# Turning attention probabilities on VectorE and by transfer instead of on TensorE, in a block-sparse attention with a channel-mix layer

## The chip, the core and the metric

One core of one Trainium2 chip runs the whole program. The metric is the device time of one execution in microseconds; lower is better. The median of three runs of the kernel before is 576.97 us (575.19 to 577.18).

## What is computed

Batch 4, 8 heads, 768 positions, head size 64, in float32. Attention is block-sparse with blocks of 32 positions (24 blocks): a query block sees the first and the last block, itself and its two neighbours, and three sampled blocks; the first and last query blocks see everything. What follows is a channel-mix layer over 512 channels with 1024 hidden units.

```python
mask = np.abs(blk_i - blk_j) <= 1
mask = mask | (blk_i == 0) | (blk_j == 0) | (blk_i == 23) | (blk_j == 23)
for qb in range(24):
    for kb in sampled_blocks[qb]:
        mask[qb*32:(qb+1)*32, kb*32:(kb+1)*32] = True
scores = np.where(mask, 0.125 * (q @ k.T), -1e9)
attn = np.exp(scores - scores.max(-1)); attn = attn / attn.sum(-1)
x = (attn @ v).transpose(0, 2, 1, 3).reshape(4, 768, 512)
xk = mu_k * x + (1 - mu_k) * x_prev      # x_prev: x one position earlier
xr = mu_r * x + (1 - mu_r) * x_prev
k = np.maximum(xk @ w_k, 0)
out = sigmoid(xr @ w_r) * (k * k @ w_v)
```

## The kernel before

**Units and tiles.** Attention runs as 24 units, counted from 0: two wide ones (the first and last query blocks of a pair of batches, `load_wide`, `wide_pair`) and 22 gathered ones (`load_near`, `near_unit`), each for two query blocks of two batches, so that 128 partitions are 4 x 32 queries. In names, `s_8_1` is the scores of gathered unit 8 of its batch pair, head group 1. The channel mix runs over 12 tiles of 128 positions (two batches each): `gate` (matmuls `r`), `hidden` or `hidden_of_two` (`h`) and `values` (`v`), each product as three float32r terms.

**A gathered unit.** For each of two groups of four heads: 32 small matmuls write scores `s` to PSUM (L609); four VectorE instructions (`soft`, L558) add the mask, take the minimum of the negated scores and write to `p` in SBUF; four ScalarE instructions (`exp`, L567) put exponentials in place. `p` has queries on its partitions, and the product with V needs keys there, so `turn` transposes it: TensorE transposes four 128x128 blocks into a PSUM tile `t` (L578), VectorE copies that tile to `pt` (L584), twice per group. Then 64 small matmuls (L640) multiply by V. From unit 8 on (`MERGE`) both groups' scores are one planned step, and so are both products. `finish` (L692) divides by the sums and transposes the result into the channel mix's input.

The softmax writes `p` through two views, and that order decides which partition a probability has after the transposition:

```python
dealt = lambda x: x.rearrange("p (g x a) -> p x a g", g=2, a=QB)
```

**Buffers.** One key buffer (`KR_BUFS` 1), six value buffers (two pairs in use per unit), four `p` buffers (`P_BUFS`), four `pt`, two PSUM tiles `t`, one PSUM bank `m` for the channel mix's results (`BANKS`; the last five tiles take more).

**The order.** Each step goes to `plan.add(engine, ns, rank, fn, reads, writes, ...)`. `Plan.order` places steps by a model of engines, buffers and transfers, and among those that can start takes the lowest rank; each engine then runs its steps strictly in the order that comes out. Ranks come from tables (`UNIT_AT`, `TILE_AT`) and offsets (`O_TR`, `LEAD_K`, ...). All loads and stores of the steady part are issued by SyncE (SP), in the planned order too; a transfer that has to wait holds up those behind it.

Of the kernel before, what the change touches and what calls it, by code (L numbers as in the profile page):

```python
# [19 lines left out]
P = 128  # L20
# [6 lines left out]
TT = 128  # L27
# [244 lines left out]
def block_sparse_attention_channel_mix(  # L272
# [31 lines left out]
    near_mask = fixed([P, NM, SLOTS], F32, "near_mask")  # L304
# [9 lines left out]
    def mask_setup():  # L314
# [21 lines left out]
        def twice():  # L336
            v = nc.vector
            c = con.ap[:, near:].bitcast(F32)
            v.tensor_copy(out=near_mask.ap, in_=c[:, NM * SEEN :].rearrange("p (a b) -> p a b", b=SLOTS))
# [13 lines left out]
            m = near_mask.ap[:, :, 0 : 2 * NRAND - 1 : 2]  # L353
            v.scalar_tensor_tensor(out=m, in0=s_, scalar=-FAR, in1=m, op0=ALU.mult, op1=ALU.add)

        plan.add(DVE, 2900, TWICE, twice, reads=[(con,)], writes=[(f,), (same,), (near_mask,)])
# [20 lines left out]
    def weight(i, owner, key, dst, src, rank):  # L377
        f = buf([P, 512], F32, "zr", Z_BUFS, f"wf{i}")
        if wide:
            raw = Part(early, EARLY_W, lambda x, i: x[:, 1024 * i : 1024 * (i + 1)].bitcast(I32).rearrange("p (a b) -> p a b", b=2)) if i < 3 * CC else buf([P, 512, 2], I32, "p", P_BUFS, f"raw{i}")  # L380
            mag = buf([P, 512], F32, "kk", 2, f"wmag{i}")
            at = RAW_AT + RAW_GAP * i if i < 3 * CC else rank
# [45 lines left out]
    def weights():  # L428
# [9 lines left out]
        for i, job in enumerate(jobs):  # L438
            late = i - 3 * CC
            weight(i, *job, rank=W0 + W1 * i + (V0 + V1 * late if late >= 0 else 0.0))  # L440
# [22 lines left out]
    def load_wide(pr, at, step):  # L463

        q = buf([P, HP, P], F32, "q", 2, f"qw{pr}")
        lead = (pr, ALL) == UNITS[0]
        for lo, hi in ((0, 1), (1, HP)) if lead else ((0, HP),):
            plan.add(SP, ISSUE, -60 + 1.5 * lo if lead else at - LEAD_Q, lambda lo=lo, hi=hi: nc.sync.dma_start(q.ap[:, lo:hi], qw[pr, :, lo:hi]),
                     writes=[(q, *range(lo, hi))], release=at - LEAD_Q, size=wire(65536 * (hi - lo), 512 * (hi - lo)))
        keys, values = [], []  # L470
        for hp in range(HP):
            keys.append([])
            values.append([])
            for i in range(PAIR):
                r = Part(k_ring, K_RING, lambda x, i: x[:, i])
                keys[-1].append(r)
                due = -59 + hp + 0.1 * i if lead else at + step * hp - LEAD_W
                if lead and not hp:
                    half = S // 2
                    for h in range(2):  # L480
# [6 lines left out]
                         writes=[(r, 0), (r, 1)], release=due, size=wire(393216, 3072))  # L487
            for i in range(PAIR):
                r = Part(v_ring, V_RING, lambda x, i: x[:, i])
                values[-1].append(r)  # L490
                due = -58.5 + hp + 0.1 * i if lead else at + step * hp - LEAD_X
                plan.add(SP, ISSUE, due, lambda r=r, hp=hp, i=i: nc.sync.dma_start(r.ap, vw[pr, hp, :, i]),
                         writes=[(r,)], release=due, size=wire(393216, 3072))
        return q, keys, values

    def load_near(pr, m, at):
# [5 lines left out]
        ahead = FIRST_K if (pr, m) == (0, 0) else LEAD_K  # L502
# [507 lines left out]

T_ACT = ((0, 1, 2), (2,))

BANKS = [("m", M_BUFS)]
LAST, XT_BUFS = 5, 6
WARM = 10
MERGE = 8
# [92 lines left out]
```

## Time and profile before

| | |
|---|---|
| median of 3 runs | 576.97 us |
| the profiled execution | 577.41 us, of which its span (first to last instruction) 575.5 us |
| TensorE busy | 541.6 us, 94% |
| VectorE, ScalarE, GpSimd busy | 302.0, 283.9, 301.8 us (49 to 52%) |
| transfers | 108.50 MB; the main queue 56.1% of 16 engines' span |

A busy share says how long an engine had work in it. Whether more could go through it is read from what it did between. A group of matmuls in the timeline starts while the one before it drains, so its cost is the distance from its start to the next start, not its own duration.

### The profile page before, as it was taken

How to read it: one execution, taken by the hardware profiler on the slowest of the kernel's cores; microseconds unless marked ns; L12 is line 12 of the kernel's file. 1: busy time of each engine (PE TensorE's matmuls, PEld its weight loads, DVE VectorE, ACT ScalarE, POOL GpSimd, SP SyncE). 2: the span in 40 equal slices, each digit the busy share in tenths (PEclk: the TensorE clock that was granted, in tenths of full speed). 3: DMA queues.
4: the chain of work that ended last, by engine and by line, in shares of the span. 5: the costliest groups of instructions: out<-in, count | busy, mean ns of one | idle time of the engine just before them, and what ended most of it. 6: DMA issues, size and time to landing. Idle time of an engine off the chain costs nothing.

```text
span 575.5 us, 18197 instructions
## 1 busy us (share of the span) xinstructions
PE 541.6 (94%) x7139; PEld 441.1 (77%) x7139; DVE 302.0 (52%) x818; ACT 283.9 (49%) x703; POOL 301.8 (52%) x368
## 2 busy tenths in 40 slices
PE   7978657898999999999999999999999999999997
PEld 3555434787789779888878888878989888888886
DVE  1887787877777673755467455556222313232001
ACT  3576664468366752744646455565324243422520
POOL 0067544868547345444406644415717879767820
PEclk8999787998999999999999999999999999999999
DMA  8999989998877887875785655484320000000001
GB/s 329 338 363 351 331 305 298 303 308 253 298 231 235 258 268 226 248 229 190 222 273 159 200 185 187 159 272 115 119 83 21 19 20 0 19 36 19 0 19 55
DMA packets 53942, 108.50 MB, mean 189 GB/s; under 512 B 9505, under 2 KB 28578, under 8 KB 53858
## 3 DMA queue, kind: packets, MB, share of 16 engines
q1 hardware_dynamic: 53570, 106.96, 56.1%
q8 instruction: 56, 0.92, 0.6%
q10 hardware_dynamic: 288, 0.39, 0.2%
q14 instruction: 28, 0.23, 0.1%
HBM read 100.77 MB, written 6.55 MB: 187 GB/s over the span
## 4 chain that ended last, share of the span: by engine, by line
PE 75%; DMA 6%; DVE 3%; SPq 2%; issue 1%; POOL 1%
PE v L898 23%; PE o L640 7%; PE s L609 5%; PE t L578 5%; PE r_1p L838 5%; PE h_3p L864 4%; PE r_0p L838 4%; PE h_0p L864 4%; PE h_1p L864 4%; PE h_2p L864 4%; DMA VR<-vt 2%; DMA KR<-kt 2%; DMA VR<-vn 1%; PE tx L703 1%; DVE p L558 1%; PE h_2p L880 1%
## 5 line engine op out<-in xcount | busy, mean ns | idle before, releaser
L898 PE MATMUL v<-wv,k 128*128 128x512 f32 (+1 forms) x600 | 140.9, 389 | 0.0
L898 PEld LDWEIGHTS v<-wv,k 128*128 128x128 f32 x600 | 108.2, 188 | 26.8 <-issue 1.2
L567 ACT ACTIVATE p<-p,nm 128x256 f32<-128x256 f32 x176 | 87.3, 498 | 31.4 <-DVE nm L558 31.2
L558 DVE CUSTOM_DVE_ANT_1 p<-s,near_mask 128x256 f32<-128x256 f32 x176 | 89.7, 632 | 19.2 <-PE s L609 19.0
L584 DVE COPY pt<-t 128x512 f32<-128x512 f32 x88 | 59.1, 686 | 67.2 <-PE t L578 54.1
L578 PE MATMUL t<-ident,p 128*128 128x128 f32 x352 | 52.0, 279 | 7.1 <-DVE pt L584 3.7
L640 PE MATMUL o<-VR,pt 128*32 128x64 f32 x2816 | 48.6, 228 | 5.9 <-DMA VR<-vt 5.1
L640 PEld LDWEIGHTS o<-VR,pt 128*32 128x32 f32 x2816 | 44.2, 115 | 11.5 <-issue 6.2
L578 PEld LDWEIGHTS t<-ident,p 128*128 128x128 f32 x352 | 41.5, 143 | 14.8 <-ACT ptw L582 3.9
L609 PE MATMUL s<-KR,q 64*32 64x256 f32 x1408 | 48.8, 402 | 4.3 <-DMA KR<-kt 4.3
L814 POOL TENSOR_TENSOR xr<-xr_1f,xr 128x256 fp32r<-128x256 f32 x24 | 17.9, 745 | 58.6 <-ACT xr L812 58.1
L805 DVE SCALAR_TENSOR_TENSOR xr_1f<-xr_1d,mk,xt 128x128 f32<-128x128 f32 x48 | 18.3, 423 | 50.3 <-POOL xr L814 42.8
L906 DVE SCALAR_TENSOR_TENSOR z<-v,z 128x512 f32<-128x512 f32 (+1 forms) x25 | 16.8, 671 | 52.8 <-PE v L898 36.8
L609 PEld LDWEIGHTS s<-KR,q 64*32 64x32 f32 x1408 | 27.5, 111 | 18.1 <-issue 5.8
L805 DVE SCALAR_TENSOR_TENSOR xr_0f<-xr_0d,mk,xt 128x128 f32<-128x128 f32 x48 | 20.0, 457 | 26.2 <-POOL xr L814 15.9
L567 ACT ACTIVATION_READ_ACCUMULATOR p<-p,nm 128x1 f32 x176 | 32.9, 187 | 0.0
L838 PE MATMUL r_0p<-wr,xr 128*128 128x512 f32 x120 | 31.2, 404 | 0.0
L838 PE MATMUL r_1p<-wr,xr 128*128 128x512 f32 x120 | 30.5, 401 | 0.0
L801 POOL TENSOR_TENSOR xr_0d<-xt 128x128 f32<-128x128 f32 x48 | 20.3, 442 | 18.0 <-DVE xr_0f L805 5.2
L814 POOL TENSOR_TENSOR xr<-xr_0f,xr 128x256 fp32r<-128x256 f32 x24 | 17.7, 738 | 21.1 <-ACT xr L812 21.1
L558 DVE DVE_READ_ACCUMULATOR2_ANT nm<- 128x1 f32 x176 | 28.3, 161 | 0.0
L812 ACT CAST xr<-xr_1f 128x256 fp32r<-128x256 f32 x24 | 9.7, 405 | 35.4 <-PE r_0p L838 16.9
(168 smaller groups left out, 1005.3 us busy)
## 6 DMA issues: line engine op xcount, KB each, us to landing
VR<-vn SPq DMA_DIRECT2D x44, 512.0 KB, 4.8
VR<-vt SPq DMA_DIRECT2D x138, 128.0 KB, 3.8
KR<-kt SPq DMA_DIRECT2D x132, 128.0 KB, 3.5
KR<-kd SPq DMA_DIRECT2D x22, 512.0 KB, 5.1
v_ring<-vw SPq DMA_DIRECT2D x16, 384.0 KB, 5.8
out<-z SPq DMA_DIRECT2D x23, 256.0 KB, 2.2
q<-qn SPq DMA_DIRECT2D x22, 256.0 KB, 3.8
k_ring<-kw SPq DMA_DIRECT2D x14, 384.0 KB, 6.4
```

The source lines that it names most:

```text
L558: nc.vector.tensor_tensor_reduce(out=dealt(p.ap[:, cs]), in0=cut(view()), in1=by, scale=-SCALE, scalar=3e38 if first is None else nm.ap[:, ...
L567: plan.add(ACT, 378 + 0.83 * (cs.stop - cs.start), rank, lambda: nc.scalar.activation(p.ap[:, cs], p.ap[:, cs], AF.Exp, bias=nm.ap[:, col ...
L578: nc.tensor.transpose(tp.ap[:, i, :], cs(p.ap), ident.ap)
L584: plan.add(DVE, 690, rank + 0.1, lambda: nc.vector.tensor_copy(out=pt.ap, in_=tp.ap), reads=[(tp,)], writes=[(pt,)])
L609: nc.tensor.matmul(s.ap[ROWS[j], row, a * 256 : (a + 1) * 256].rearrange("p (x a g) -> p g a x", g=2, a=QB), q.ap[half, hp, ROWS[j]], eigh ...
L640: nc.tensor.matmul(o.ap[ROWS[j], h * D : (h + 1) * D], held[gi][i // 2].ap[:, 2 * (i % 2) + g, ROWS[j]], VR[values[j % PAIR][g]].ap[:, j / ...
L801: sub.tensor_tensor(out=part(d.ap), in0=x.ap[:, two, c, 1 : 1 + TT], in1=x.ap[:, two, c, 0:TT], op=ALU.subtract)
L805: nc.vector.scalar_tensor_tensor(out=part(f.ap[:, i, :]), in0=part(d.ap), scalar=mk.ap[:, which, c : c + 1], in1=x.ap[:, two, c, 0:TT], op ...
L814: plan.add(POOL, 80 + 2.4 * MIX * tw, rank + O_MIX, lambda f=f, cs=cs: nc.gpsimd.tensor_tensor(out=dst.ap[:, 1, cs], in0=f.ap, in1=dst.ap[ ...
L838: nc.tensor.matmul(pr.ap[:, 0:512], xr.ap[:, a, c, :], wr.ap[:, w, c, :], start=(c == 0 and m == 0), stop=(c == CC - 1 and m == 2))
L864: nc.tensor.matmul(ph.ap[:, ff * PAIR * TT : (ff + 1) * PAIR * TT], wk.ap[:, w, c, f * P : (f + 1) * P], xk.ap[:, a, c, :], start=(c == 0 ...
L898: nc.tensor.matmul(pv.ap[:, 0:width], hid[f][2](a), wv.ap[:, w, f, cs], start=(f == 0 and m == 0), stop=(f == FC - 1 and m == 2))
```

## The change

For units 8 to 23 (`CARRY`), 16 of the 22 gathered ones, `turn` is not called. `soft` writes `p` with keys in another order, `carry` has VectorE transpose each 32x32 block of `p` (128x1024, one instruction) into a new tile `tb` of the `p` kind, and SP then issues four transfers from SBUF to SBUF that move 32 partitions x 4 KB of `tb` back to 128 partitions x 1 KB of `p`. The product with V reads `p`. The mask gets a second copy in the new order. From tile 3 on the channel mix's results may also take the PSUM tiles `t`. And everything is planned anew: the offsets before are replaced by tables with one number per unit for keys and values, per weight for loads and conversions, and all other ranks have new numbers.

```diff
             if inner:
-                by = mask().unsqueeze(1).to_broadcast([P, BLK, SLOTS]).rearrange("p x (a g) -> p x a g", g=2)
-                cut = lambda x: x.rearrange("p (x a g) -> p x a g", g=2, a=QB)
-                dealt = lambda x: x.rearrange("p (g x a) -> p x a g", g=2, a=QB)
+                by = mask().unsqueeze(1).to_broadcast([P, BLK, SLOTS])
+                cut = lambda x: x.rearrange("p (x y) -> p x y", y=SLOTS)
+                if blocks:
+                    dealt = lambda x: x.rearrange("p (y x) -> p x y", x=BLK)
+                else:
...
+    def carry(p, keys, name, rank):
+
+        turned = buf([P, 4 * 256], F32, "p", P_BUFS, f"tb{name}")
+        plan.add(DVE, 1250, rank, lambda: nc.vector.transpose(
+            out=turned.ap.rearrange("p (k y c) -> p k y c", k=QB, c=BLK), in_=p.ap.rearrange("p (y k c) -> p k y c", k=QB, c=BLK)),
+            reads=[(p, *keys)], writes=[(turned,)])
+
+        def away():
+            for r in (0, 2, 1, 3):
+                nc.sync.dma_start(p.ap[:, r * 256 : (r + 1) * 256], turned.ap[r * BLK : (r + 1) * BLK])
+
+        plan.add(SP, QB * ISSUE, rank + 0.05, away, reads=[(turned,), (p, *keys)], writes=[(p, *keys)], size=QB * wire(180000, 1024), parts=QB)
...
+            if carried:
+                every = [(i, i * 256) for i in range(4)]
+                carry(p, every, f"{b}_{m}_{gi}", at + O_TR)
+                held.append(([(p, *every)], lambda i, g, j, pt=p: pt.ap[:, j * 256 + (2 * i + g) * BLK : j * 256 + (2 * i + g + 1) * BLK]))
+                continue
...
-        plan.add(SP, ISSUE, at - LEAD_Q, lambda: nc.sync.dma_start(q.ap, qn[pr, m]),
-                 writes=[(q, *range(HP))], release=at - LEAD_Q, size=wire(262144, 2048))
+        plan.add(SP, ISSUE, keys_at - 1, lambda: nc.sync.dma_start(q.ap, qn[pr, m]),
+                 writes=[(q, *range(HP))], release=keys_at - 1, size=wire(262144, 2048))
...
-        tags = BANKS
+        tags = [("m", M_BUFS)] if tile_now[0] < SHARED else [("m", M_BUFS), ("t", T_BUFS), ("t", T_BUFS)]
...
+CARRY = 8
+SHARED = 3
...
+KEYS_AT = [
+    -10.1028, -44.6072, 30.887, -99.6782, 55.0175, 65.6048, 75.2198, 80.1323, 92.2395,
```

**TensorE between the products with V of units 0_7 and 0_8.** In these rows `v`, `r`, `h` are the channel mix's matmuls, `t` the transpositions of probabilities, `tx` those of `finish`, `s` scores and `o` products with V. Before, from the last matmul of `o_7`:

```order
L640 MATMUL o_7_3006<-VR_71,pt_7_1_1_2802 32x64
L838 MATMUL r_1_1p<-wr,xr_1_1_2566 128x512 x6
L578 MATMUL t_8_0_0_3096<-ident,p_8_0_2974 128x128 x4
L838 MATMUL r_1_1p<-wr,xr_1_1_2566 128x512 x6
L703 MATMUL tx_7_3113<-ident,x_7_3094 128x128 x4
L578 MATMUL t_8_0_1_3123<-ident,p_8_0_2974 128x128 x4
L609 MATMUL s_9_0_3130<-KR_69,q_9_2775 32x2x4x32 x16
L609 MATMUL s_9_1_3157<-KR_69,q_9_2775 32x2x4x32 x16
L898 MATMUL v_128_0_3180<-wv,k_1_2777 128x512 x21
L578 MATMUL t_9_1_0_3256<-ident,p_9_1_3188 128x128 x4
L898 MATMUL v_128_0_3180<-wv,k_1_2777 128x512 x3
L578 MATMUL t_9_1_1_3266<-ident,p_9_1_3188 128x128 x4
```

Now, the same place, up to the first matmul of `o_8`:

```order
L664 MATMUL o_7_3028<-VR_71,p_7_1_2749 32x64
L922 MATMUL v_128_0_3103<-wv,k_1_2731 128x512 x24
L628 MATMUL s_9_0_3153<-KR_69,q_9_1429 32x8x32 x16
L628 MATMUL s_9_1_3171<-KR_69,q_9_1429 32x8x32 x16
L862 MATMUL r_2_0p<-wr,xr_2_0_3000 128x512 x12
L727 MATMUL tx_7_3231<-ident,x_7_3120 128x128 x4
L664 MATMUL o_8_3238<-VR_72,p_8_0_2875 32x64
```

No `t` stands there any more, and `o` reads `p` itself.

**SP at the same place** (`VR` are the value buffers, `KR` the key buffer; `VR_74` is loaded for unit 0_8). Before:

```order
L539 DMA VR_74<-vt 32x1024
L539 REGISTER_ALU x2
L539 ISA
L539 DMA VR_74<-vt 32x1024
L532 DMA VR_71<-vn 128x1024
```

Now:

```order
L540 DMA VR_74<-vt 32x1024
L540 REGISTER_ALU x2
L540 ISA
L540 DMA VR_74<-vt 32x1024
L613 DMA p_8_1_3100<-tb_8_1_3141 128x1x256 x4
L933 DMA out<-z_1_1_2975 128x512
L509 DMA KR_69<-kd 128x1024
```

The four transfers of a group stand between loads; here the keys of unit 0_10 are behind those of group `p_8_1`.

## Rows read from the trace of the kernel before

**Rows 1.** Page, part 1: one engine's busy time, share, instructions.

```profile
PE 541.6 (94%) x7139; PEld 441.1 (77%) x7139; DVE 302.0 (52%) x818; ACT 283.9 (49%) x703; POOL 301.8 (52%) x368
```

**Rows 2.** Windows: length; busy PE, PEld, DVE, ACT, POOL; PEclk, DMA share, GB/s.

```profile
0.00:150.00 150.00, 119.73 (x1911) 86.23 (x1919) 108.32 (x290) 89.09 (x213) 78.74 (x86) 0.91 0.92 317
...
50.00:100.00 50.00, 34.14 (x619) 23.32 (x618) 37.38 (x94) 28.61 (x78) 26.29 (x24) 0.80 0.94 311
...
150.00:400.00 250.00, 249.79 (x4078) 210.67 (x4065) 150.62 (x444) 136.48 (x379) 114.59 (x149) 1.00 0.69 220
400.00:446.00 46.00, 46.00 (x608) 41.71 (x597) 14.75 (x31) 17.99 (x37) 26.93 (x32) 1.00 0.23 73
446.00:576.00 130.00, 126.13 (x567) 102.50 (x565) 28.27 (x58) 40.30 (x75) 81.56 (x103) 1.00 0.06 21
```

**Rows 3.** Timeline, TensorE, 80 to 140 us: start, duration, [idle before, releaser].

```profile
85.82 1.06 PE L609 MATMUL s<-KR,q 64*32 64x256 f32 x4 [2.28 <-DMA KR<-kt]
...
139.19 3.59 PE L640 MATMUL o<-VR,pt 128*32 128x64 f32 x126 [1.83 <-DMA VR<-vt]
```

**Rows 4.** Windows with line L578 alone: PE busy and count of transpositions.

```profile
150.00:450.00 300.00, 36.38 (x260) 30.38 (x260) 1.00 0.61 194
```

**Rows 5.** Timeline, TensorE, 227 to 263 us.

```profile
227.67 1.96 PE L609 MATMUL s<-KR,q 64*32 64x256 f32 x64
229.56 3.10 PE L864 MATMUL h_3p<-mixed,wk 128*128 128x256 f32 x24
232.50 1.03 PE L578 MATMUL t<-ident,p 128*128 128x128 f32 x8
233.47 1.99 PE L640 MATMUL o<-VR,pt 128*32 128x64 f32 x128
235.39 3.07 PE L838 MATMUL r_1p<-wr,xr 128*128 128x512 f32 x12
238.29 0.60 PE L578 MATMUL t<-ident,p 128*128 128x128 f32 x4
...
256.08 0.60 PE L578 MATMUL t<-ident,p 128*128 128x128 f32 x4
256.51 0.60 PE L703 MATMUL tx<-ident,x 128*128 128x128 f32 x4
256.93 5.88 PE L898 MATMUL v<-wv,k 128*128 128x512 f32 x24
262.65 0.60 PE L578 MATMUL t<-ident,p 128*128 128x128 f32 x4
```

**Rows 6.** Chain that ended last: start, duration, what (matmuls after matmuls).

```profile
435.20 2.80 PE h_1p L864 x24
```

**Rows 7.** Timeline, VectorE, 229 to 236 us: softmax steps, then two copies.

```profile
229.74 0.63 DVE L558 CUSTOM_DVE_ANT_1 p<-s,near_mask 128x256 f32<-128x256 f32 x1 [1.27 <-PE s L609]
...
231.66 0.63 DVE L558 CUSTOM_DVE_ANT_1 p<-s,near_mask 128x256 f32<-128x256 f32 x1
...
235.08 1.29 DVE L584 COPY pt<-t 128x512 f32<-128x512 f32 x2 [1.38 <-PE o L640]
```

**Rows 8.** Timeline, ScalarE: the fourth exponential of that group.

```profile
232.30 0.19 ACT L567 ACTIVATION_READ_ACCUMULATOR p<-p,nm 128x1 f32 x1
```

**Rows 9.** Groups by line: the copies; count, busy, mean ns, idle before.

```profile
L584 DVE COPY pt<-t 128x512 f32<-128x512 f32 x88 | 59.1, 686 | 67.2 <-PE t L578 54.1 <-PE o L640 12.5 <-PE tx_-1_940 L703 0.3
```

**Rows 10.** Timeline, SP: a store's issue, then three loads.

```profile
249.42 0.38 SPq L909 DMA_DIRECT2D out<-z  x1
...
253.87 2.12 SPq L539 DMA_DIRECT2D VR<-vt  x3
```

**Rows 11.** Page, part 6, and the tile view of KR: issue to landing.

```profile
KR<-kt SPq DMA_DIRECT2D x132, 128.0 KB, 3.5
...
DMA to landing us min/median/max: 2.2/3.7/8.3
```

**Rows 12.** Waits of SP's queue: who waited for whom, total, times, longest.

```profile
SPq L532 <- PE o L640: 25.3, 7, 9.0
```

More of the change, by code (lines that the diff above doesn't have):

```diff
@@ L461, in sampled_block, with load_wide @@
         return (sampled[n] >> (5 * j)) & (ROOM - 1)
-    def load_wide(pr, at, step):
+    def load_wide(pr, i, step):
+        n, at = i, KEYS_AT[i]
         q = buf([P, HP, P], F32, "q", 2, f"qw{pr}")
@@ L476, in load_wide @@
                 keys[-1].append(r)
-                due = -59 + hp + 0.1 * i if lead else at + step * hp - LEAD_W
+                due = -59 + hp + 0.1 * i if lead else at + step * hp
                 if lead and not hp:
@@ L486, in load_wide @@
                 plan.add(SP, ISSUE, due, lambda r=r, hp=hp, i=i: nc.sync.dma_start(r.ap, kw[pr, hp, :, i]),
-                         writes=[(r, 0), (r, 1)], release=due, size=wire(393216, 3072))
+                         writes=[(r, 0), (r, 1)], release=max(due, 0.0), size=wire(393216, 3072))
             for i in range(PAIR):
@@ L507, in load_near @@
         slots[0][r] = pr
-        plan.add(SP, ISSUE, at - ahead, lambda: nc.sync.dma_start(
+        plan.add(SP, ISSUE, keys_at, lambda: nc.sync.dma_start(
             K.ap[:, WINDOW : WINDOW + 4].rearrange("p n b x -> p (n b x)"), kd[pr, :, n - 1 : n + 3].rearrange("p n x -> p (n x)")),
-            writes=[(K, "near")], release=at - ahead, size=wire(524288, 4096))
+            writes=[(K, "near")], release=keys_at, size=wire(524288, 4096))
         for j in range(PAIR):
@@ L520, in fetch @@
                                       kt[bass.ds(sampled_block(n + j, i) + pr * NB, 1)].rearrange("o p x -> p (o x)"))
-            plan.add(SP, NRAND * FETCH + FIND * (pr == 0) + ISSUE * more, at - ahead + 0.01 * j, fetch, reads=[(packed,)],
-                     writes=[(K, ("far", j))], release=at - ahead, size=wire(131072, 1024) * (NRAND + 2 * more), parts=NRAND + more)
+            plan.add(SP, NRAND * FETCH + FIND * (pr == 0) + ISSUE * more, keys_at + 0.01 * j, fetch, reads=[(packed,)],
+                     writes=[(K, ("far", j))], release=keys_at, size=wire(131072, 1024) * (NRAND + 2 * more), parts=NRAND + more)
         for j in range(PAIR):
@@ L596, in eight, with near_unit @@
         return replace(x, ap=[list(x.ap[0]), [apart, 2], [block, QB], [1, BLK]])
-    def near_unit(b, m, together, q, keys, values, o, L, t0, t1):
+    def carry(p, keys, name, rank):
[7 more added lines that the diff above has]
+        plan.add(SP, QB * ISSUE, rank + 0.05, away, reads=[(turned,), (p, *keys)], writes=[(p, *keys)], size=QB * wire(180000, 1024), parts=QB)
+    def near_unit(b, m, together, carried, q, keys, values, o, L, t0, t1):
         scores, held = [], []
@@ L1011 @@
 T_ACT = ((0, 1, 2), (2,))
-BANKS = [("m", M_BUFS)]
 LAST, XT_BUFS = 5, 6
@@ L1052 @@
+WEIGHT_AT = [
+    -20.8248, -53.2243, -52.6791, 13.0687, -45.5517, 21.6385, 4.801, 37.1423, 19.7861,
+    43.5324, 12.8773, 50.241, -13.5655, -74.8683, 54.4146, 116.3902, 92.3941, 67.0115,
+    107.6012, -38.0923,
+]
+CONVERT_AT = [
+    -150.3153, -81.7926, -164.2279, -22.1667, -20.6773, 9.2581, -29.1155, 15.5374, 8.9153,
+    17.1985, 47.2794, 52.7703, 49.9036, -14.0758, 56.4673, 158.3134, 65.1365, 73.8086,
+    76.8627, 55.3873,
+]
+T_RATE = 1.5576
 def kernel(**inputs):
```

99 lines of the change are left out of this document (53 added, 46 removed).

## The prediction

> **What bounds the kernel now.** I read the windows first, because a mean over the span hides stages. TensorE is busy 119.73 of the first 150 us, then 249.79 of 250 and 46 of 46, and 126.13 of the last 130 [rows 2]. So there are two stages. [...] After 150 us TensorE has work without a gap at clock 1.00, and VectorE (150.62 of 250), ScalarE (136.48) and GpSimd (114.59) are far from full [rows 2]; over the span they stand at 49 to 52%, TensorE at 94% [rows 1]. In that second stage a microsecond taken out of TensorE's queue should move the end by a microsecond, as long as nothing that TensorE needs comes later than now. The stage is not at a rate limit of another engine: the question is only latency.
>
> **What is removed from TensorE.** The 16 units have two groups of eight transpositions each: 256, in 64 groups of four. Three ways to price them. Start to start, four cost 0.43 us (256.08 to 256.51) and eight 0.97 (232.50 to 233.47) [rows 5]: 64 x 0.43 = 27.5 at least, 32 x 0.97 = 31.0 at most. The line's busy time from 150 to 450 us is 36.38 us for 260 [rows 4]; that counts their overlap with the next group too, so 35.8 for 256 is a ceiling. Beside the group itself there is the change of kind: 24 `h` matmuls cost 2.94 us from their start to that of the transpositions behind them [rows 5], and 2.80 between matmuls of the same kind [rows 6]. The order of before has these 64 groups in 48 separate places, so up to 48 x 0.14 = 6.7 us more. I take 28 + 4 = **32 us**, bounds 27.5 and 35.8.
>
> The rest of TensorE's work stays: the same scores, products with V and channel mix. The score matmuls write another layout of PSUM, and the products read `p` where they read `pt`; both have the same counts, and I cost them at nothing, since TensorE's queue is the same length.
>
> **What is added elsewhere.** VectorE loses 64 copies of 686 ns [rows 9], 43.9 us, and gets 32 block transpositions of 128x1024. No row has one. Below, one copy of 512 elements, 0.69 us; above, four softmax steps of 256 elements, 1.92 us (229.74 to 231.66) [rows 7]; nearest is two copies for the same 1024 elements, 1.29 us [rows 7]. I take 1.29: 41 us. So VectorE's total is about what it was (22 to 61 us added, 44 removed), and at 150.62 of 250 us [rows 2] even the upper end doesn't bind. The softmax writes `p` in another stride; before, its neighbouring elements already fell far apart, so I keep 0.48 us a step. The second mask copy is one small instruction before the units begin.
>
> The transfers are 128 of 131 KB, 16.8 MB. While transfers are busy, the kernel moves 220/0.69 = 319 GB/s [rows 2], which makes 53 us of all 16 engines; at half that rate 105 us. Idle transfer time between 150 and 446 us is 0.31 x 250 + 0.77 x 46 = 113 us [rows 2], so both ends fit, the second one barely. [...]
>
> SP gets 128 issues. A store's issue takes 0.38 us, a load with a computed address 0.71 (three in 2.12) [rows 10]: 49 us at 0.38, on a queue that now issues some 17 transfers for a unit. What matters more is that each group of four waits for VectorE, and that loads queue behind it, as the keys of unit 0_10 do behind `p_8_1`. Those keys need the one key buffer, which the scores of 0_9 leave only 7.6 us after the product of unit 0_7 ends; the transposition is over before that (next part). So here the wait costs nothing.
>
> **The new chain, and what covers it.** A carried group holds two of the four `p` buffers until its product with V. So the second group of unit u+1 can't start its softmax before the product of unit u is done, and its whole chain lies between those two products: hop and four softmax steps and their exponentials, 2.75 us (229.74 to 232.49, the end of the fourth exponential) [rows 7, 8]; 1.29 for the transposition; four issues, the last 3 x 0.38 = 1.1 us after the first; landing 2.2 to 3.7 us after that (shortest and median of 128 KB key loads, longest 8.3) [rows 11]; 0.3 us for semaphores. Sum: **7.6 to 9.1 us**; 13.7 with the longest landing. The cover is what TensorE has in its queue between the two products, from the new order and the prices of [rows 5]: from unit 0_7 to 0_8 it is 5.72 (`v`) + 1.89 (`s`) + 2.90 (`r`) + 0.43 (`tx`) = 10.9 us, the least of all. The fifteen covers of units 0_7 to 1_10 are 19.7, 10.9, 14.0, 21.0, 12.1, 31.6, 15.9, 13.2, 12.4, 13.8, 19.0, 18.9, 13.9, 13.8 and 21.7. So in the undisturbed case nothing waits. But the value loads of the next unit start at the same moment, since they too wait for the product of u, and they stand ahead on SP: a pair is 0.9 MB, 2.8 us at 319 GB/s, and now and then SP already waits up to 9.0 us for such a product [rows 12]. I put down 4 us in all for places where the chain comes late, bounds 0 and 20.
>
> [...]
>
> **The first stage.** All transfers are planned anew there. Ahead of the keys of the seventh gathered unit (0_6) SP issues 43.9 MB before and 45.1 MB now, by the sizes of the order's rows; at 317 GB/s [rows 2] that is 3.8 us later if transfers set the pace. Against it, TensorE has 15 `v` matmuls fewer ahead of that unit's scores (3.6 us, which come behind them instead). And the 30.3 us of idle time and the 0.91 clock leave room for gain. I take 0, bounds -8 and +6.
>
> **The last stage.** After the last product with V only the channel mix is left. What is due there is less (some 93 us by the order, 130 before [rows 2]), because attention and mix are spread over each other longer; the sum of work is the same, and the same `v` matmuls end it. I cost this and the wider choice of PSUM tiles at nothing; it is covered as long as TensorE's queue is full.
>
> **Sum.** Span 575.5 - 32 + 4 + 0 = 547.5; with the 1.9 us around it 549.4 for a profiled execution. That execution (577.41) lies 0.4 us over the median, so the forecast is **549 us**. Its own range from the bounds: least 577 - 35.8 - 8 = 533, most 577 - 27.5 + 20 + 6 = 575; not all at once, so 538 to 561.
>
> **Rivals.**
> *Late at some units* (about 566 us): a chain of about 14 us, that is the longest landing, or the lower transfer rate with the value loads ahead, in most units. Stalls at 14 us: 3.1 + 1.9 + 0.8 + 1.6 + 0.2 + 0.1 + 0.2 = 8 us; at 15.5 us 20. For: [rows 11, 12]. Against: transfers are idle 31% of that stage [rows 2]. By itself it gives 549 - 4 + 8 = 553 to 565, with the slower first stage up to 571; 566 stands for its upper part, since the lower lies in the forecast's own range.
> *The chain takes the place of the transpositions* (slower): if it costs c, over 15.9 us, nine of the covers fall short, by 9c - 120 us together (120 is their sum). That equals the 32 us saved at c = 16.9. At 18 us, which needs landings of the longest kind for two of the four transfers in a row, or SP standing some 9 us [rows 12] ahead of the four issues in each unit, 42 us are lost: 549 - 4 + 42 = **587 us**. Against: the sum of 7.6 to 9.1.
> *No change* (574 to 580): the wait moves from TensorE's queue to transfers, c near 17. It takes the middle of the two, and I see no row that puts it there.
> *The first stage gains* (under 538): the idle 30.3 us falls by over 8. Nothing in the order ahead of unit 0_6 shows fewer bytes.
>
> **Chances.** Forecast 538 to 561: 0.66. Late at some units: 0.16. No change: 0.05. Slower: 0.08. First stage gains: 0.05. A measurement of this kernel tells 0.5% from no change, about 3 us. Faster: 0.66 + 0.16 + 0.05 = 0.87; same 0.05; slower 0.08. Range 538 to 566: it holds the forecast's case and most of the late one, and leaves out about 0.2.
>
> **What would show it.** Right: no transposition rows of units 0_6 on, TensorE over 98% busy from 150 us to the end, and the product with V preceded by idle time only in a few places; about 27 to 36 us less of line 578's kind; block transpositions near 1.3 us; `p` transfers landing in 2.2 to 3.7 us. Wrong: products that wait for the `p` transfers by 2 us or more at the units with covers under 14 us (0_8, 1_0, 1_3, 1_4, 1_5, 1_8, 1_9), SP rows that wait long for VectorE in front of key loads, a granted clock under 1.00 after 150 us, or a front stage longer than 156 us to the scores of unit 0_6.

## The result, and the profile after

The changed kernel takes **583.2 us** (median of 4 runs, 581.2 to 584.5) against 577.1 us for the kernel before: a ratio of 1.0104, 95% interval 1.0061 to 1.0147. It is slower by about 1%; 549 us were forecast. The profiled execution took 583.11 us, its span is 581.3 us. Medians here and below are of undisturbed executions: one of 989.55 us beside three of 558.65 to 563.54 us, for instance, is left out, and so three medians (574.7, 573.1 and 559.3 us) stand a little under those that later expectations quote (575.2, 573.4 and 561.4 us).

Part 1 of the page answers to [rows 1]: TensorE is busy for only 17 us less, where 256 matmuls fewer should take off 27.5 at least, and its share fell from 94% to 90%.

```profile
PE 524.7 (90%) x6883; PEld 413.0 (71%) x6883; DVE 301.3 (52%) x787; ACT 289.5 (50%) x707; POOL 298.1 (51%) x368
```

The windows answer to [rows 2], with the same columns:

```profile
0.00:150.00 150.00, 119.21 (x1951) 80.22 (x1952) 107.68 (x292) 89.51 (x213) 74.84 (x83) 0.94 0.91 314
...
150.00:400.00 250.00, 230.07 (x3297) 191.17 (x3296) 130.58 (x342) 126.35 (x329) 125.01 (x163) 0.99 0.78 237
400.00:446.00 46.00, 43.84 (x662) 34.97 (x666) 23.11 (x67) 24.97 (x66) 24.23 (x29) 0.96 0.76 225
```

The first 150 us are as they were (119.21 us busy, 119.73 before). The damage is in the stage that had no gap: 20 us of TensorE's time are idle between 150 and 400 us, where 0.2 were. The waits of TensorE between 150 and 480 us (who waited for whom: total, times, longest) name transfers above all:

```profile
PE o L664 <- DMA p<-tb: 5.4, 8, 1.6
PE h_1p L888 <- issue: 3.2, 1, 3.2
PE s L628 <- DMA KR<-kt: 3.1, 2, 2.3
PE s L628 <- DMA p<-tb: 2.9, 1, 2.9
PE o L664 <- DMA VR<-vt: 2.6, 2, 2.0
```

Not only the moved probabilities are late (`p<-tb`), but keys (`KR`) and values (`VR`) as well. Over the whole stretch from 150 to 480 us TensorE idles 22.5 us. The rows that are left run some 10 us longer than before (27.5 us at least were taken out, and the busy time fell by 16.9). I put that down to short waits inside a group, as in the 60 matmuls at 243.07 us below, and to the granted clock, which was 1.00 after 150 us before and is now 0.99 from 150 to 400 us and 0.96 from 400 to 446 us; how much each takes was not measured.

**Why the keys are late.** The chain of work that ended last, near 230 us (start, duration, what):

```profile
225.04 0.48 SPq L540
...
227.67 0.60 SPq L613
228.36 0.58 SPq L613
...
232.27 0.56 SPq L613
232.92 0.55 SPq L509
...
238.00 0.34 SPq L520
238.68 4.26 DMA KR<-kt
...
243.07 3.21 PE s L628 x60
```

`SPq` is the queue of SyncE (SP), L540 value loads, L613 the four transfers of a group, L509 to L520 the keys. From 225 to 238 us the critical path is nothing but SyncE issuing one transfer after another: eight issues of the change in a row, 0.65 us apart, and the keys behind them. TensorE's timeline shows who pays; 64 such matmuls took 1.96 us in [rows 5]:

```profile
240.16 0.62 PE L628 MATMUL s<-KR,q 64*32 64x256 f32 x4 [0.80 <-DMA KR<-kt]
243.07 3.21 PE L628 MATMUL s<-KR,q 64*32 64x256 f32 x60 [2.29 <-DMA KR<-kt]
```

**Why the probabilities are late.** One group, on three engines. VectorE's timeline: the block transposition ends at 351.71, and the next one, at 363.51, has waited 6.19 us for a buffer that transfers still hold:

```profile
350.46 1.25 DVE L607 STREAM_TRANSPOSE tb<-p 128x1024 f32<-128x1024 f32 x1
...
363.51 1.25 DVE L607 STREAM_TRANSPOSE tb<-p 128x1024 f32<-128x1024 f32 x1 [6.19 <-DMA p<-tb]
```

SyncE's timeline: it gets to the four issues at 358.50, 6.8 us after the transposition, since value loads stand ahead; the fourth is out at 361.09:

```profile
351.96 0.54 SPq L533 DMA_DIRECT2D VR<-vn  x1
352.77 2.24 SPq L540 DMA_DIRECT2D VR<-vt  x3
355.05 0.58 SPq L533 DMA_DIRECT2D VR<-vn  x1
356.25 2.15 SPq L540 DMA_DIRECT2D VR<-vt  x3
358.50 2.59 SPq L613 DMA_DIRECT2D p<-tb  x4
361.17 0.55 SPq L509 DMA_DIRECT2D KR<-kd  x1
```

TensorE's timeline: the product waits for the landing, twice:

```profile
362.53 0.30 PE L664 MATMUL o<-VR,p 128*32 128x64 f32 x4 [0.46 <-DMA p<-tb]
363.47 1.08 PE L664 MATMUL o<-VR,p 128*32 128x64 f32 x58 [0.64 <-DMA p<-tb]
```

I paired the 32 transpositions with the 32 groups of issues in their order. From the end of the transposition to the end of the fourth issue it takes 7.2 us in the mean (median 5.9, longest 17.8), and to the last landing 9.3 us (longest 19.8). VectorE stands 41.2 us for `p` buffers that transfers hold, in its waits of that stretch:

```profile
DVE tb L607 <- DMA p<-tb: 23.8, 6, 6.2
...
DVE p L564 <- DMA p<-tb: 17.4, 4, 7.5
```

The transfers themselves are not slow. The tile view (duration ns least/median/largest) and part 6 of the page, which answers to [rows 11]:

```profile
L613 SPq DMA_DIRECT2D p<-tb x128: 549/584/1815, 160.9 to 472.5; - x128
L607 DVE STREAM_TRANSPOSE tb<-p x32: 1229/1245/1262, 152.6 to 468.3; 128x1024 f32<-128x1024 f32 x32
...
DMA to landing us min/median/max: 2.5/2.8/4.3
```

```profile
KR<-kt SPq DMA_DIRECT2D x132, 128.0 KB, 3.6
p<-tb SPq DMA_DIRECT2D x128, 128.0 KB, 2.8
```

How full SyncE is can be counted from its timeline: issues, with gaps of up to 0.7 us between them (register rows of 29 to 44 ns in the median at L540, semaphore rows of 17 at L613) counted as busy, as us of each 50:

| kernel | 150-200 | 200-250 | 250-300 | 300-350 | 350-400 | 400-450 |
|---|---|---|---|---|---|---|
| before | 42 | 44 | 37 | 31 | 32 | 10 |
| after | 46 | 49 | 40 | 44 | 47 | 44 |

The number of issues between 150 and 480 us went from 267 to 397, and the waits in the list of SyncE's queue for that stretch fell from 112.7 us in all to 48.6. Of those 48.6, 22.7 are at L613 itself, 35 waits of at most 3.9 us: SyncE also stands in front of the change's transfers until they may start.

### The profile page after: what moved, and what is told of

The parts are those of the page before. It is cut to its first block, busy times and chain, and to the rows that moved or that the text cites. A ratio compares the mean times of both kernels' runs of the same rounds, so it can differ in the third digit from the quotient of the medians.

```text
span 581.3 us, 17991 instructions
## 1 busy us (share of the span) xinstructions
PE 524.7 (90%) x6883; PEld 413.0 (71%) x6883; DVE 301.3 (52%) x787; ACT 289.5 (50%) x707; POOL 298.1 (51%) x368
## 3 DMA queue, kind: packets, MB, share of 16 engines
q1 hardware_dynamic: 72002, 123.75, 66.9%
## 4 chain that ended last, share of the span: by engine, by line
PE 56%; DMA 18%; SPq 11%; ACT 5%; issue 4%; DVE 4%; POOL 1%; DVEq 0%; ACTq 0%; POOLq 0%
PE v L922 18%; PE s L628 5%; DMA p<-tb 5%; PE o L664 5%; DMA k_ring<-kw 4%; SPq L540 4%; PE r_1p L862 3%; PE r_0p L862 3%; PE h_1p L888 3%; ACT p L573 3%; DMA KR<-kt 2%; DMA VR<-vt 2%; SPq L520 2%; SPq L613 2%; PE h_3p L888 2%
## 5 line engine op out<-in xcount | busy, mean ns | idle before, releaser
L564 DVE CUSTOM_DVE_ANT_1 p<-s,near_mask 128x256 f32<-128x256 f32 x176 | 91.1, 628 | 56.7 <-PE s L628 28.5
L628 PE MATMUL s<-KR,q 64*32 64x256 f32 x1408 | 52.3, 412 | 11.2 <-DMA KR<-kt 8.0
L607 DVE STREAM_TRANSPOSE tb<-p 128x1024 f32<-128x1024 f32 x32 | 39.8, 1243 | 29.1 <-DMA p<-tb 23.8
L664 PE MATMUL o<-VR,p 128*32 128x64 f32 x2048 | 36.6, 220 | 8.4 <-DMA p<-tb 5.4
L664 PEld LDWEIGHTS o<-VR,p 128*32 128x32 f32 x2048 | 31.4, 110 | 15.3 <-DMA p<-tb 8.2
L825 POOL TENSOR_TENSOR xr_1d<-xt 128x128 f32<-128x128 f32 x48 | 19.3, 420 | 29.1 <-DVE xr_0f L829 17.3
L417 POOL TENSOR_TENSOR wf<-wf,early 128x512 f32<-128x512 f32 x8 | 10.4, 1295 | 40.4 <-DVE wf L406 31.2
L829 DVE SCALAR_TENSOR_TENSOR xr_1f<-xr_1d,mk,xt 128x128 f32<-128x128 f32 x48 | 17.9, 413 | 22.6 <-POOL xr L838 19.8
L888 PE MATMUL h_1p<-mixed,wk 128*128 128x256 f32 x192 | 26.3, 293 | 3.2 <-issue 3.2
L888 PEld LDWEIGHTS h_1p<-mixed,wk 128*128 128x128 f32 x192 | 25.0, 200 | 4.1 <-issue 3.3
```

The source lines that it names most:

```text
L564: nc.vector.tensor_tensor_reduce(out=dealt(p.ap[:, cs]), in0=cut(view()), in1=by, scale=-SCALE, scalar=3e38 if first is None else nm.ap[:, ...
L607: plan.add(DVE, 1250, rank, lambda: nc.vector.transpose(out=turned.ap.rearrange("p (k y c) -> p k y c", k=QB, c=BLK), in_=p.ap.rearrange(" ...
L628: nc.tensor.matmul(s.ap[ROWS[j], row, a * 256 : (a + 1) * 256].rearrange("p (x g a) -> p g a x" if carried else "p (x a g) -> p g a x", g= ...
L664: nc.tensor.matmul(o.ap[ROWS[j], h * D : (h + 1) * D], held[gi][1](i, g, j), VR[values[j % PAIR][g]].ap[:, j // PAIR, h * D : (h + 1) * D] ...
L825: sub.tensor_tensor(out=part(d.ap), in0=x.ap[:, two, c, 1 : 1 + TT], in1=x.ap[:, two, c, 0:TT], op=ALU.subtract)
L829: nc.vector.scalar_tensor_tensor(out=part(f.ap[:, i, :]), in0=part(d.ap), scalar=mk.ap[:, which, c : c + 1], in1=x.ap[:, two, c, 0:TT], op ...
```

## The experiments

Four theories stood at the start, on some 29 us that had to be explained (583.2 less the 554.2 of the first run below): **A**, VectorE's queue stands for buffers that the transfers hold; **B**, SyncE has no time for four more issues a group, so that loads, transfers and all that waits for them come late; **C**, the added bytes slow the other transfers; **D**, the new tables of numbers give a worse order, whatever turns the probabilities. Where nothing else is said, an edit is made in the changed kernel and leaves every other instruction at its place. Times are medians; the ratio is to the kernel before on the same chip, with its 95% interval. The kernel before took 577.1 to 578.9 us on these chips, so a difference between two runs' medians is good to some 2 us.

**Everything but the transfers.** In `away`:

```diff
-            for r in (0, 2, 1, 3):
-                nc.sync.dma_start(p.ap[:, r * 256 : (r + 1) * 256], turned.ap[r * BLK : (r + 1) * BLK])
+            pass
```

> The four transfers of every group are left out; the block transposition stays, the products read probabilities that were not moved, and every other instruction keeps its place on its engine. Theories: A, VectorE's queue stands still for buffers that the transfers hold (41.2 us of such waits in the profile of after); B, the transfers' four issues of 0.65 us each on SyncE make keys, values and the transfers themselves late; C, their 16.8 MB slow the other transfers; D, the waits belong to the new tables of numbers, whatever turns the probabilities. A, B and C together: all of the second stage's added idle time and short waits (about 32 us) ends, 549 to 556 us. D: 570 us or more.

Measured 554.2 us, ratio 0.9557 (0.9492 to 0.9623). Block transpositions, new order and new masks stay, and the kernel is 29.1 us faster than with transfers. TensorE is busy for 326.21 of the 330 us from 150 to 480 us, after the change 307.54. So A, B and C together hold the whole loss.

**The tables alone.**

```diff
-CARRY = 8
+CARRY = 24
```

> The change's tables of numbers and its third use of banks, but TensorE transposes the probabilities of all units as before and no transfer is made. D: the new order is bad by itself, and with 28 to 32 us of transpositions back on TensorE it takes 585 to 610 us. A to C: the new order is about as good as the old one, 570 to 582 us.

Measured 581.9 us, ratio 1.0069 (1.0038 to 1.0100). D in its full form is out, but the new order with TensorE's transpositions is 4.6 us slower than the old one by these medians, at the upper end of what A to C allowed. Against the run above it also gives the price of what was taken from TensorE: 581.9 - 554.2 = 27.7 us (the two orders were planned apart).

**The buffer let go early.** The four transfers read constant weights instead of `tb`:

```diff
-                nc.sync.dma_start(p.ap[:, r * 256 : (r + 1) * 256], turned.ap[r * BLK : (r + 1) * BLK])
+                nc.sync.dma_start(p.ap[:, r * 256 : (r + 1) * 256],
+                                  wr.ap.rearrange("p a c x -> p (a c x)").bitcast(F32)[r * BLK : (r + 1) * BLK, 0:1024])
```

> The four transfers of every group read rows of the constant weights instead of the turned probabilities: issues, bytes and landings stay, the product still waits for them, but the buffer of the turned probabilities comes free when the transposition ends; the real probabilities are left out. A: the 41 us of VectorE's waits for transfers all but end and, by the share of them that reached TensorE, 563 to 573 us. B, C and D: 580 to 586 us, since nothing on SyncE, in the bytes or in the tables is different.

Measured 574.7 us, ratio 0.9950 (0.9913 to 0.9987): 8.5 us of 29, short of what A alone wanted (563 to 573). VectorE's waits for these transfers are gone from its list; the product's are not.

**No bytes.** Each transfer moves 1 KB:

```diff
-                nc.sync.dma_start(p.ap[:, r * 256 : (r + 1) * 256], turned.ap[r * BLK : (r + 1) * BLK])
+                nc.sync.dma_start(p.ap[0:BLK, r * 256 : r * 256 + 8], turned.ap[r * BLK : (r + 1) * BLK, 0:8])
```

> Each of the four transfers moves 32 partitions of 8 elements instead of 32 rows of 1024 elements into 128 partitions: as many issues, the same waits and the same buffers held, but 1 KB instead of 128 KB; most of the move is left out. C: the bytes are the cause, 555 to 567 us. A, B and D: a landing only some tenths of a us shorter, 576 to 583 us.

Measured 576.5 us, ratio 0.9980 (0.9933 to 1.0028): not C's 555 to 567. Landing still takes 2.1 us (median), 2.8 with 128 KB.

**Both at once**: 1 KB from the constant weights.

```diff
-                nc.sync.dma_start(p.ap[:, r * 256 : (r + 1) * 256], turned.ap[r * BLK : (r + 1) * BLK])
+                nc.sync.dma_start(p.ap[0:BLK, r * 256 : r * 256 + 8],
+                                  wr.ap.rearrange("p a c x -> p (a c x)").bitcast(F32)[r * BLK : (r + 1) * BLK, 0:8])
```

> Both edits at once: the four transfers of a group read 8 elements a row of the constant weights, so neither the turned buffer is held by them nor are their bytes moved; the four issues on SyncE and the product's wait for its own transfers stay; the real probabilities are left out. Alone the two edits gave 575.2 and 576.5 us of 583.2. A and C (buffers and bytes are two separate causes, and the rest is B): the sum of the two, 566 to 571 us. B alone (issues and landing; the two edits only shorten the same waits): 573 to 576 us. A and C alone, with nothing left for B: 553 to 558 us.

Measured 573.1 us, ratio 0.9919 (0.9881 to 0.9957), beside 574.7 and 576.5 alone: the two don't add up, they shorten the same waits. Without bytes and without held buffers, 19 of the 29 us are still there. What is left of the change's transfers is their issues, SyncE's wait in front of them and the product's wait.

**One transfer a group.**

```diff
-            for r in (0, 2, 1, 3):
-                nc.sync.dma_start(p.ap[:, r * 256 : (r + 1) * 256], turned.ap[r * BLK : (r + 1) * BLK])
+            nc.sync.dma_start(p.ap[:, 0:256], turned.ap[0:BLK])
```

> One transfer for each group instead of four (the first one, 128 KB); the other three quarters of the probabilities are not moved. SyncE then spends about 0.65 us for a group instead of 2.6 and the last landing comes about 2 us earlier; the turned buffer is still held until the landing. B (the issues): 558 to 566 us. A (the hold of the buffer, whose length is mostly the landing of 2.8 us): 572 to 578 us. C (three quarters of the bytes gone): about 578 us.

Measured **553.7 us**, ratio 0.9595 (0.9529 to 0.9660): as without any, and lower than B expected. One transfer of 128 KB a group, with its landing (median 3.0 us), its hold of the buffer and the product's wait, costs nothing. So neither the hold nor the landing costs anything by itself; what they cost in the changed kernel needs more than one transfer a group. SyncE's timeline at the place where eight issues stood:

```profile
226.75 0.56 SPq L612 DMA_DIRECT2D p<-tb  x1
227.40 1.22 SPq L533 DMA_DIRECT2D VR<-vn  x1
```

**Two transfers a group.**

```diff
-            for r in (0, 2, 1, 3):
+            for r in (0, 2):
```

> Two of the four transfers of a group are made; half of the probabilities are not moved. One transfer gave 553.7, four gave 583.2. If each transfer costs for itself (its bytes, its hold, its wait): a straight line between them, 561 to 566 us. If SyncE runs full: nothing until its queue is full, then all, 553 to 559 us.

Measured 559.3 us, ratio 0.9705 (0.9611 to 0.9799). None, one, two, four: 554.2, 553.7, 559.3, 583.2. The first is free, the second costs 6 us, the third and fourth 12 us each. I read that as the bend of a queue that fills up, though a softer one than "nothing until its queue is full, then all".

**Issues that nobody waits for.** Four transfers of 1 KB from the weights to memory that isn't read:

```diff
-                nc.sync.dma_start(p.ap[:, r * 256 : (r + 1) * 256], turned.ap[r * BLK : (r + 1) * BLK])
+                none = dr.tile([BLK, 8], F32, name=f"none{name}_{r}")
+                nc.sync.dma_start(none, wr.ap.rearrange("p a c x -> p (a c x)").bitcast(F32)[r * BLK : (r + 1) * BLK, 0:8])
```

> In the place of each group's four transfers SyncE issues four transfers of 32 x 8 elements from the constant weights to memory that nobody reads: no product waits for them, no buffer is held by them, 1 KB each. The probabilities are not moved. What is left of the change's transfers is SyncE's time alone, four issues for a group at the same places. B as the whole cause (SyncE has no time left between 150 and 450 us): 570 to 577 us, close to the 573.4 us of the run in which the product still waits. If the product's own wait for its transfers is what the 573.4 us were made of: 553 to 558 us, as without transfers.

Measured 562.3 us, ratio 0.9765 (0.9707 to 0.9822), between the two forecasts: SyncE's time alone, by way of loads that come later, costs 8 us. It is a lower bound, because these issues are shorter (median 420 ns; 584 for those of the change) and because SyncE doesn't stand in front of them until the transposition is done (0.6 us of such waits between 150 and 480 us; 18.1 with 1 KB from the weights). The step from here to 573.1 us, 11 us, is that standing and the product's wait for transfers that were issued late, which no run separates; from there to 583.2, held buffers and bytes, 10 us.

**The price in the planner.**

```diff
-        plan.add(SP, QB * ISSUE, rank + 0.05, away, ...
+        plan.add(SP, QB * 660, rank + 0.05, away, ...
```

> The planner counts 660 ns for each of the four transfers on SyncE instead of 450, and orders the work by it; nothing else is different, and all of the work stays. If only the order on SyncE was bad (the planner put loads behind issues that it took for shorter): 563 to 573 us. If SyncE's time itself is missing: 577 to 585 us.

Measured 584.9 and 580.5 us, two executions only, beside 583.2. The planner's order with the true price of the issues is no better, which speaks for time that is missing and not only misplaced; other tables of numbers were not tried with it.

**The old tables.** The kernel before, with the carrying alone added and its own tables and banks kept:

```diff
+                carry(p, every, f"{b}_{m}_{gi}", at + O_MAX + 0.1)
...
-                near_unit(b, m, i >= MERGE, q, keys, values, o, L, t0, t0 + SECOND)
+                near_unit(b, m, i >= MERGE, i >= CARRY, q, keys, values, o, L, t0, t0 + SECOND)
...
+CARRY = 8
```

Its block transposition is due right after the softmax, not at `O_TR` as in the change.

> The kernel before with its own tables of numbers and its own use of banks, and only the carrying of probabilities from the 9th gathered unit on added; the planner orders the work with the old numbers. D (the new tables are the cause): 545 to 570 us. A to C: the same waits come with any tables, 575 to 595 us.

Measured 609.4 us, ratio 1.0535 (1.0457 to 1.0612), so D is wrong the other way round: with the old tables, and that one rank, the change costs more. Here SyncE's count is 48, 50, 50, 49 and 48 of 50 from 200 to 450 us. From its timeline:

```profile
300.79 3.16 SPq L613 DMA_DIRECT2D p<-tb  x4
304.04 0.54 SPq L509 DMA_DIRECT2D KR<-kd  x1
304.84 4.04 SPq L520 DMA_DIRECT2D KR<-kt  x6
308.99 1.31 SPq L933 DMA_DIRECT2D out<-z  x1
310.36 0.42 SPq L500 DMA_DIRECT2D q<-qn  x1
310.87 2.50 SPq L613 DMA_DIRECT2D p<-tb  x4
```

SyncE's rows in a timeline never name a wait. Its list of waits for 200 to 450 us has none over 1.5 us: here it is an engine that hardly stops.

**Other queues.** Four ways to take issues from SyncE. Two of a group's four by ScalarE:

```diff
-                nc.sync.dma_start(p.ap[:, r * 256 : (r + 1) * 256], turned.ap[r * BLK : (r + 1) * BLK])
+                (nc.sync if r < 2 else nc.scalar).dma_start(p.ap[:, r * 256 : (r + 1) * 256], turned.ap[r * BLK : (r + 1) * BLK])
```

> Two of the four transfers of each group are issued by ScalarE's queue instead of SyncE's; every bit of the work stays. B: SyncE is free 1.3 us earlier for each group and the group's last issue comes 1.3 us earlier, so 572 to 579 us, if ScalarE, which must wait for the block transposition before it issues, loses nothing. Rival: ScalarE stands in that wait with exponentials and GELUs queued behind it, 583 to 595 us. A, C and D: 581 to 585 us.

Measured 584.2 us, ratio 1.0091 (1.0055 to 1.0126). The time fits two forecasts, ScalarE standing in the wait and A, C or D, and doesn't tell them apart. SyncE is a little freer (37 to 48 of 50 us between 150 and 450, against 40 to 49), but its list of waits has a new kind: loads that stand for the change's transfers. The planner keeps a limit on bytes under way by making a load wait for an earlier transfer, and those that ScalarE issues land 4.1 us after their issue in the median, SyncE's own after 3.1.

```profile
SPq L520 <- DMA p<-tb: 9.2, 3, 4.1
```

All four by GpSimd:

```diff
-                nc.sync.dma_start(p.ap[:, r * 256 : (r + 1) * 256], turned.ap[r * BLK : (r + 1) * BLK])
+                nc.gpsimd.dma_start(p.ap[:, r * 256 : (r + 1) * 256], turned.ap[r * BLK : (r + 1) * BLK])
```

> All four transfers of each group are issued by GpSimd's queue instead of SyncE's, at the same places of the planned order; bytes, buffers, waits and all of the work stay. If SyncE's full queue makes the whole loss: 556 to 568 us. If the transfers under way make it, whoever issues them: 578 to 586 us. Rival: GpSimd, busy for half of the span, stands before the transposition with mixing work queued behind it: 585 to 600 us.

Measured 576.9 us, ratio 0.9985 (0.9952 to 1.0019), between the forecasts. Keys and values are late no longer (0.2 and 0.3 us left in TensorE's list); but now GpSimd, with mixing work queued behind, stands in front of the issues until the transposition is done:

```profile
POOL p L613 <- DVE tb L607: 16.6, 6, 6.0
```

The same, with the planner told so:

```diff
-        plan.add(SP, QB * ISSUE, rank + 0.05, away, ...
+        plan.add(POOL, QB * 1000, rank + 0.05, away, ...
```

> The transfers are issued by GpSimd and the planner knows it (1000 ns of GpSimd for each, an estimate from nothing better than the 0.65 us on SyncE), so it orders all engines anew; all of the work stays. If SyncE's queue makes the loss: 553 to 568 us, the better the more GpSimd's waits are planned around. If the transfers under way make it: 578 to 590 us.

Measured 589.3 us, ratio 1.0172 (1.0099 to 1.0245), and that wait grew to 28.9 us. It lies in the range given to "the transfers under way". But in this order the fourth issue ends only 2.8 us after the transposition in the mean (7.2 in the changed kernel), and TensorE's waits from 150 to 480 us name transfers for 7.9 us and results of ScalarE, VectorE and GpSimd for 19.0. So late issues aren't what makes it slow; what in the order does **stays open**.

Two by GpSimd (r = 0, 2) and two by SyncE:

```diff
-                nc.sync.dma_start(p.ap[:, r * 256 : (r + 1) * 256], turned.ap[r * BLK : (r + 1) * BLK])
+                (nc.sync if r % 2 else nc.gpsimd).dma_start(p.ap[:, r * 256 : (r + 1) * 256], turned.ap[r * BLK : (r + 1) * BLK])
```

> Two of a group's four transfers are issued by GpSimd's queue and two by SyncE's, at the same places of the order; all of the work stays. If the series of four issues on one queue makes the loss: each queue now has the two of the run with two transfers (561.4 us), so 561 to 570 us. If each queue that is added only brings its own waits, as with ScalarE (584.2) and GpSimd alone (576.9): 576 to 584 us.

Measured **567.4 us**, ratio 0.9817 (0.9779 to 0.9855). All of the work is done, and it beats both kernels: 16 us under the change, 11 under the kernel before. Bytes and buffers are those of the change, and the landings are even longer than its 2.8 us (part 6 of the page):

```profile
p<-tb POOLq DMA_DIRECT2D x64, 128.0 KB, 4.2
p<-tb SPq DMA_DIRECT2D x64, 128.0 KB, 4.1
```

But the series of issues on one queue is halved, the fourth one ends 4.9 us after the transposition in the mean, and the list of TensorE's waits from 150 to 480 us names no `p<-tb` any more. That is the strongest evidence for B in the wider sense: 16 of the 29 us went when that series was halved, so they are the time that four issues take one after another on one queue, together with what that queue does besides. Some 13 us stay lost against no transfers at all.

**Through memory and back.** Two issues of 512 KB, `there<-tb` and `p<-there`, in the place of four:

```diff
+        plan.add(SP, ISSUE, rank + 0.05, lambda: nc.sync.dma_start(there.ap, turned.ap), ...
+        plan.add(SP, ISSUE, rank + 0.1, lambda: nc.sync.dma_start(
+            p.ap.rearrange("q (r c) -> q r c", r=4), there.ap.rearrange("(r i) (k c) -> i k r c", r=4, k=4).rearrange("i k r c -> (i k) r c")), ...
```

> The probabilities of a group go to memory in one transfer of 512 KB and come back in another one that deals the rows out, instead of four transfers inside SBUF: two issues on SyncE instead of four, twice the bytes, two landings one after the other; the planner orders the two apart. All of the work stays. B: 1.3 us of SyncE's time less for each group, 556 to 566 us. C (bytes): 585 us or more. The landings one after the other (the chain of one group of some 12 us against covers of 10 to 30 us): 575 to 590 us.

Measured 619.7 us, ratio 1.0741 (1.0683 to 1.0799), worse than any case of mine. Halving the issues didn't help where SyncE had to stand for the first landing, with all loads behind it:

```profile
SPq L614 <- DMA there<-tb: 75.2, 22, 6.3
```

**Half of the groups**, with SyncE, then with two queues as above, then without transfers:

```diff
-CARRY = 8
+CARRY = 16
```

> Only the units from the 17th on are carried (16 groups of 32), in the change's tables; the planner orders the work anew; all of the work stays. B (SyncE full): half of the added issues, in the half of the stage where SyncE had most time left in the kernel before, so each carried group brings its 0.86 us: 581.9 less 13.7, 566 to 573 us. A, C or the products' own wait, which hold for each group alone: as all 32 groups brought nothing against TensorE's transpositions in the same tables (583.2 against 581.9), 580 to 584 us.

> As before, but only the units from the 17th on are carried (16 groups), in the order of the run that carried those by SyncE alone and took 578.6 us; all of the work stays. The transpositions saved are half of 27.7 us from 581.9, 568 us if nothing is lost. If the series on one queue makes the loss: 568 to 574 us. If the transfers make it, whoever issues them: 577 to 581 us.

> The kernel that carries 16 groups, in its own planned order, with the transfers left out (the probabilities of those groups are not moved). If its order is as good as the others in these tables: half of 27.7 us below 581.9, 566 to 570 us, and the 16 groups' transfers cost 8 to 12 us. If the order is worse by itself: 574 to 579 us, and the transfers cost next to nothing there.

Measured 578.6 us (1.0021, 0.9986 to 1.0056), 578.3 (1.0003, 0.9967 to 1.0039) and 568.7 (0.9862, 0.9818 to 0.9907). The order is as good as the others, and the 16 groups' transfers cost 9.9 us. I had expected SyncE to have room there. It hasn't: its count is 50 and 47 of 50 between 350 and 450 us, and the fourth issue ends 6.4 us after the transposition in the mean, nearly as with 32 groups. Two queues bring nothing here (578.3 us, the range given to the transfers, "whoever issues them"), where they bring 16 us with 32 groups. TensorE's waits from 150 to 480 us hardly name transfers with either queueing: 2.9 of 10.9 us with SyncE and 1.3 of 9.1 with two queues; the rest are results of VectorE, ScalarE and GpSimd. For 16 groups SyncE is therefore not shown to be the cause, and what delays those results **stays open**.

More `p` buffers, the plain way to end VectorE's waits, weren't tried, nor was a single issue for a group inside SBUF.

## Why the prediction was wrong, point by point

**What bounds the kernel**: right. The second stage was TensorE's alone, and 27.7 us came out of the time when the transpositions went and nothing else came (554.2 us). But I called it a question of latency only and wrote that the stage is "not at a rate limit of another engine". The windows that I read list no SyncE. It was at 42 and 44 of 50 us already before the change, by the table above.

**Removed from TensorE**: 32 us were put down, 27.7 measured between two orders planned apart, at the lower bound of 27.5. The 4 us for the changes of kind didn't show.

**VectorE**: right. A block transposition takes 1.245 us (1.29 assumed), the softmax steps 628 ns, and VectorE's busy time is 301.3 us, 302.0 before.

**Bytes**: right. Landings are 2.8 us (2.2 to 3.7 assumed), those of keys are as before. From the run with one transfer a group (61.7% of a span of 551.4 us in the main queue) to the changed kernel (66.9% of 581.3) 96 transfers took 48.7 us of all 16 engines, so 128 take an estimated 65: between my 53 and 105.

**SyncE's issues**: here the sum failed first. I took 0.38 us from a store [rows 10] and 49 us in all, though plain value loads (`VR<-vn`) of the kernel before took 0.53 us in the median; measured are 0.58 us and a gap, 0.65, which makes 83 us on a queue that had 64 us free between 150 and 400 us and 40 in the next 50, by the table above: room only if every issue found a gap. I weighed one case where the keys stand behind a group, found that the key buffer wasn't free yet, and wrote "the wait costs nothing"; at 232.92 us the same pattern made TensorE stand.

**The new chain**: the step that failed. Its term "four issues, the last 3 x 0.38 = 1.1 us after the first" took a SyncE that is free when the transposition ends. Measured from the end of the transposition to the end of the fourth issue are 7.2 us in the mean and 17.8 at most, and 9.3 and 19.8 to the last landing. With that, and the first and last terms as I had them, the chain is 2.75 + 1.25 + 9.3 + 0.3 = 13.6 us in the mean instead of 7.6 to 9.1, and up to 24, against covers of 10.9 to 31.6. No run shows the 0.3 us for semaphores, an estimate of mine; in the chain that ended last after the change, a product starts 0.04 us after the landing that it waited for (430.47 to 430.51 us). The 4 us of stalls became 29. A second wait wasn't in the chain at all: the turned buffer of a group is one of the same four, held until its last transfer lands, so that VectorE stands for it with the softmax and mixing of other units behind (41.2 us). Of the signs that I had named, the granted clock fell under 1.00 after 150 us, but no product waited 2 us for its transfers (8 waits, the longest 1.6): the lateness reached TensorE in many small waits, and through keys and values.

**First and last stage**: about right. The scores of unit 0_6 start at 147.24 us in TensorE's timeline (149.79 before) with 3.6 us less work ahead of them, so the front lost some 1 us. The idle time up to 150 us, 30.3 us before [rows 2], is 30.8, at a granted clock of 0.94 (0.91). That the order itself would cost something I had not weighed; with TensorE's transpositions it is 4.6 us slower.

**The balance**: 577.1 + 4.8 (the new order, 581.9) - 27.7 (transpositions) + 29.1 (transfers) = 583.2 (583.3 by rounding). These are differences of the runs and add up by how they are made; what they tell is which term was off. I had put 577 - 32 + 4, so the transfers were mis-sized by 25 us.

**The rivals**: the slower one had the mechanism, "SP standing some 9 us [rows 12] ahead of the four issues in each unit". It got 0.08, because I held the sum of 7.6 to 9.1 us against it, in which SyncE's other issues have no term. SyncE got to the first of the four issues 4.4 us after the transposition in the mean, so its condition of 9 us wasn't met; that its 587 us is near 583.2 is partly luck, since keys and values, which it leaves out, were late too. "Late at some units" had the chain's length of about 14 us and charged 8 to 20 us for it; the measured loss is larger, since the chain's length scatters and keys and values are late too.

## What to carry to other kernels

Before work is handed to transfers, count the issuing queue like an engine: issues times their measured duration in each stretch, beside what it issues already. SyncE was busy for nine tenths of the stretch here and issues in order, so four issues of 2.6 us were out 7.2 us after the transposition in the mean, and each late transfer held a buffer and the engine that wanted it. Spreading the issues over two queues can help: it did with SyncE and GpSimd for 32 groups (567.4 us), not with ScalarE (584.2) and not for 16 groups (578.3). Every queue that then waits for another engine must be looked at for what is queued behind it.

## What the runs showed of the hardware

- An issue of a transfer inside SBUF (32 partitions of 4 KB to 128 of 1 KB) held the issuing engine for about the same time on three engines: 584 ns on SyncE, 582 on ScalarE, 558 on GpSimd (medians; spans on GpSimd are rough). With 1 KB instead of 128 KB it was 557 ns, so bytes hardly mattered to it; 1 KB to memory took 420. From issue to landing it was 2.1 us with 1 KB and 2.8 with 128 KB. One transfer a group with its landing cost nothing (553.7 us, 554.2 with none); four, on a SyncE that was at up to 49 of 50 us, cost 29.
- The same transfers of 128 KB landed later in the runs where another queue issued them, alone or beside SyncE: 2.8 us in the median with SyncE alone, 3.1 (SyncE's) and 4.1 (ScalarE's) with two queues, 4.1 and 4.2 with SyncE and GpSimd, 4.3 with GpSimd alone. Why wasn't tested.
- A 32x32 block transposition of 128x1024 numbers of 4 bytes takes 1.245 us on VectorE, less than two copies of 128x512 (1.29) [rows 7].
